# A planned attention-and-two-gated-layers kernel: the planner's costs are replaced, 157 due times are moved, k^T v is split by column halves, and two head pairs take the exponential of q row by row

## The chip, the cores and the metric

The kernel runs on one core of one Trainium2 chip. The metric is the device time of one execution in microseconds; lower is better. TensorE is PE in the rows, VectorE DVE, ScalarE ACT, GpSimd POOL and SyncE, which only issues DMAs here, SP.

## The reference

Linear attention over 4 batches, 8 heads, 576 positions and 64 columns, then two gated layers over the 2304 rows by 512 columns that come out of it, each with 1536 inner columns. Inputs of the attention are float32; the weights are 64-bit floats, so the kernel loads two 32-bit words for each weight and converts them.

```python
def _attn_ref(q, k, v):
    q_s = np.exp(q - np.max(q, axis=-1, keepdims=True))
    q_s = q_s / (np.sum(q_s, axis=-1, keepdims=True) + 1e-09)
    k_s = np.exp(k - np.max(k, axis=2, keepdims=True))
    k_s = k_s / (np.sum(k_s, axis=2, keepdims=True) + 1e-09)
    kv = np.einsum('bhsd,bhse->bhde', k_s, v)
    return np.einsum('bhsd,bhde->bhse', q_s, kv)
def _moe_ref(x, w_gate, w_val, w_out):      # first layer
    g = x @ w_gate
    return (g / (1.0 + np.exp(-g)) * (x @ w_val)) @ w_out
def _moe2_ref(x, w_a, w_b, w_out):          # second layer
    return ((x @ w_a) * (x @ w_b)) @ w_out
```

## The kernel before, in words

**Work.** A unit of attention is one batch and one pair of heads: u = 4 b + g, 16 units, written by `attend(b, g, ...)`. A unit loads k, q and v (512 main positions as 4 rows per partition, and 64 rest positions), takes the column maximum of k (transposes `kx` and `kb` on PE, a reduce on DVE), subtracts it, takes the exponential, multiplies k^T v on PE (`kv`, line 730: 4 matmuls of 130 columns for the main positions and one for the rest, both heads side by side), divides it by its sums (lines 737 to 751) and puts it into a block-diagonal matrix. q has its row maximum subtracted, its exponential taken and is divided by the row sums; it is turned on PE (`qt`, `ql`, lines 780 and 783), and `xt` and `xl` (lines 793 and 803) are the products with the block-diagonal matrix, the layer's input x.

For batch 0 (b == 0) q's maximum is subtracted on POOL (lines 698 and 702), one ACT instruction takes the exponential of k and q together (line 706, 1280 columns), DVE sums q's rows (line 756) and POOL divides (line 767). For the other batches ACT takes the exponential of q row by row: 9 instructions of line 717, each with the maximum as its bias and each followed by a read of its accumulator that gives the row's sum; POOL divides (lines 771 and 774).

**Weights.** The inner columns are cut into 12 tiles f of 128. `convert` turns the two words of each weight into one float32 in the tiles `a` (ACT lines 412 and 417; DVE lines 414 to 428; line 433 on DVE, where it is CUSTOM_DVE_ANT_0 in a profile and ISA in an order, or on POOL, where it is a TENSOR_TENSOR), and then into a high part (ACT line 438) and a low part (the helper `pair`, line 326, on DVE or POOL): the tile `w`, called w0_f for layer 0. A float32 product is made of three: low times high, high times low, high times high.

**Blocks.** Layer 0 runs over block 0 (512 rows of batch 0; tile `xhl`, split into its high and low part) and block 1 in the plain way: for each f two products `u` (gate and value, lines 844 and 859, 12 matmuls each), SiLU on ACT into `s`, the product on DVE (line 873), its high part `h` on ACT and low part on DVE, and 12 matmuls into `acc` (line 886) that trail by one tile. Units of batch 1 are attended between block 0's products, those of batches 2 and 3 between block 1's. The rest of layer 0, and all of layer 1, runs in three supers over pairs of blocks (lines 1138, 1222, 1248, 1250, 1257), where sums of halves of x and of w are multiplied. The second layer's weights are converted in block 1's and the first supers' time (`convert_late`, tiles `latewr`).

**What sets the order.** Nothing is issued when it is written: `plan.add` records each operation with an engine, a cost in microseconds, what it reads and writes, and for some a second engine with a cost of its own. `prepare` gives each operation a due time, backwards from its successors. `order` then simulates the engines: at each step it takes, of the operations that can start first, the one that is due first; an operation with two engines goes to the second where that ends no later. `HOP` and `SAME` are the delays between engines and on one, `DMA_*` the model of a load, `TABLE` of a load of ACT's tables. `search` runs this 160 times, moving about 3% of the due times by up to 3 us at random, and keeps the shortest plan. `emit` issues in the order of that plan, so the engine queues and SP's DMAs stand in it; the semaphores come from the data. The products of the layers are chained (`product`), so that their own order is fixed; what moves are the attention's PE operations between them, everything on DVE, ACT and POOL, the choice between DVE and POOL or ACT, the buffers and the loads.

Of the kernel before, what the change touches and what calls it, by code (L numbers as in the profile page):

```python
# [31 lines left out]
class Plan:  # L32
# [58 lines left out]
    def hop(self, first, then, other):  # L91

        if first != then:
            return other
        return 0.0 if first == "tensor" else self.SAME

    def prepare(self):
# [7 lines left out]
        for n in reversed(range(len(ops))):  # L105
# [4 lines left out]
            for s in self.succ[n]:  # L110
                if n in ops[s]["hold"]:
                    continue
                hop = self.hop(op["engine"], ops[s]["engine"], self.SLACK) + lands if n in ops[s]["deps"] else 0.0
                t = min(t, self.due[s] - hop)
# [5 lines left out]
    def order(self):  # L120
# [37 lines left out]
        while len(done) < len(ops):  # L158
# [25 lines left out]
            if port:  # L184
                port_free = t + cost
# [8 lines left out]
            free[engine] = t + cost  # L194
# [13 lines left out]
            for s in succ[n]:  # L208
                left[s] -= 1
                if not left[s]:  # L210
                    at = ops[s]["engine"]
                    is_ready(s, max([end[d] + self.hop(ops[d]["runs"][run[d]][0], at, self.HOP)
# [4 lines left out]
    def search(self):  # L217

        self.prepare()
        rng, best = random.Random(0), None  # L220
        for n in range(self.ROUNDS):
            kept = self.due
            if best:
                self.due = [d + rng.uniform(-3, 3) if rng.random() < 0.03 else d for d in kept]
            try:
                found = self.order()
            except RuntimeError:
                self.due = kept
                continue
            if best and self.length > best[0]:  # L230
                self.due = kept
            else:
                best = self.length, found
        return best[1]

    def emit(self):
        done, run, slot = self.search()
# [7 lines left out]
def kernel(  # L245
# [90 lines left out]
    def dma(fn, nbytes, reads, writes, due=None, after=(), issue=0.475, queue="sync", hold=()):  # L336
# [5 lines left out]
    def load(fn, nbytes, writes, issue=0.475):  # L342
# [4 lines left out]

    mats = [[m.bitcast(U32) for m in ms] for ms in ((w_gate, w_val, w_out), (w_a, w_b, w_out2))]
# [4 lines left out]
    TOP = 122880.0  # L353
    LEAST = 2.0 ** -15
# [102 lines left out]
    def convert_late(f, m):  # L457
# [23 lines left out]
        dma(get, P * 2 * WH * 8, [], [LOW, HIGH], issue=0.95 if m < 2 else 0.475, after=first)  # L481
# [46 lines left out]
    def attend(b, g, xhl, due):  # L528
# [63 lines left out]
        def qraw():  # L592
            return col(Q, q0, n)
# [781 lines left out]
```

## Time and profile before

| | |
|---|---|
| time, median of 3 runs | 942.72 us (940.71 to 944.29) |
| the profiled execution's own time | 941.4 us |
| its span | 939.2 us, so 2.2 us lie around the span |
| PE busy | 904.6 us, 4400 matmuls |
| DVE, ACT, POOL busy | 638.1, 518.3, 334.9 us |

A busy PE is counted from the start to the modelled end of each matmul, and matmuls overlap; so the starts of rows that follow each other tell more than their durations. POOL's spans are rough.

### The profile page before, as it was taken

The page shows a single profiled execution, that of the slowest core. Times are in us where ns is not written, and L with a number is a line of the kernel's source. Part 1 is how long each engine was busy: PE and PEld are TensorE (multiplying, and loading weights), DVE is VectorE, ACT ScalarE, POOL GpSimd, SP SyncE. Part 2 cuts the span into 40 slices and gives each one's busy share as a digit, 9 for nine tenths or more (in the row PEclk, how much of TensorE's full clock was granted, in tenths as well). Part 3 has the DMA queues.
Part 4 walks back from the last instruction along what each step waited for, and adds up shares of the span by engine and source line. Part 5 has one row for each costly group of instructions (what it writes and reads, how often), then busy time and mean ns, then how long its engine had stood idle before and what let it go on. Part 6 is the DMA issues. An engine that isn't in the chain of part 4 may idle for free.

```text
span 939.2 us, 12787 instructions
## 1 busy us (share of the span) xinstructions
PE 904.6 (96%) x4400; PEld 753.0 (80%) x4400; DVE 638.1 (68%) x1025; ACT 518.3 (55%) x1020; POOL 334.9 (36%) x323
## 2 busy tenths in 40 slices
PE   5599999999999999999999999999999999999998
PEld 3477777788887888888888888888888888888886
DVE  6999996544376887877778665875796444564444
ACT  4798876878675665455464546443644453333310
POOL 6534221212052322435555633442565113242210
PEclk9989999999999999999999999999999999999999
DMA  9858765464327555354322753422223210110003
GB/s 271 273 204 263 237 224 192 122 195 131 88 90 234 157 147 156 120 165 154 112 91 72 228 183 101 135 89 90 68 66 115 79 46 22 45 46 23 23 1 112
DMA packets 108153, 121.42 MB, mean 129 GB/s; under 512 B 31929, under 2 KB 83897, under 8 KB 107961
## 3 DMA queue, kind: packets, MB, share of 16 engines
q1 hardware_dynamic: 102424, 116.55, 39.7%
q10 hardware_dynamic: 5664, 4.07, 1.4%
q8 instruction: 34, 0.56, 0.2%
q14 instruction: 31, 0.25, 0.1%
HBM read 88.60 MB, written 31.98 MB: 128 GB/s over the span
## 4 chain that ended last, share of the span: by engine, by line
PE 83%; DVE 5%; ACT 4%; DMA 3%; issue 2%; SPq 1%; POOL 1%; ACTq 0%; DVEq 0%; POOLq 0%
PE p L1138 35%; PE o L1248 15%; PE u L859 10%; PE q L1222 7%; PE o L1250 6%; PE acc L886 5%; PE o L1257 2%; DMA wr<-in_moe_w_out_dram 1%; PE xt L793 1%; DVE l2w L326 1%; ACT ut L717 1%; ACT a L412 1%; PE kv L732 1%; SPq L620 1%; DMA wf<-latewr 1%
## 5 line engine op out<-in xcount | busy, mean ns | idle before, releaser
L1138 PE MATMUL p<-l2w,l2w 128*128 128x512 f32 x1512 | 352.8, 389 | 1.2 <-DVE temps L326 1.2
L1138 PEld LDWEIGHTS p<-l2w,l2w 128*128 128x128 f32 x1512 | 283.1, 188 | 61.2 <-DVE temps L326 2.5
L859 PE MATMUL u<-xhl,w 128*128 128x512 f32 x552 | 143.3, 407 | 5.0 <-DVE w L326 4.8
L326 POOL TENSOR_TENSOR l2w<-raww,l2w 128x512 fp32r<-128x512 f32 x68 | 97.2, 1434 | 94.1 <-ACT l2w L333 94.0
L333 ACT CAST l2w<-raww 128x512 fp32r<-128x512 f32 x144 | 87.9, 621 | 74.9 <-PE p L1138 39.7
L859 PEld LDWEIGHTS u<-xhl,w 128*128 128x128 f32 x552 | 101.9, 191 | 31.8 <-DVE w L326 7.1
L326 DVE TENSOR_TENSOR sums<-o,sums 128x512 f32<-128x512 f32 x120 | 82.3, 689 | 53.2 <-PE o L1248 39.4
L326 DVE TENSOR_TENSOR temps<-p,temps 128x512 f32<-128x512 f32 x90 | 62.1, 690 | 67.1 <-PE p L1138 65.9
L1248 PE MATMUL o<-l2w,hp 128*128 128x512 f32 x288 | 97.0, 391 | 0.6 <-DVE sums L326 0.6
L1150 ACT COPY temps<-p 128x512 f32<-128x512 f32 x72 | 42.4, 588 | 67.3 <-PE p L1138 67.1
L326 DVE TENSOR_TENSOR l2w<-raww,l2w 128x512 fp32r<-128x512 f32 x76 | 57.1, 762 | 26.5 <-ACT l2w L333 26.3
L886 PE MATMUL acc<-h,w 128*128 128x512 f32 x288 | 72.1, 395 | 0.0
L1222 PE MATMUL q<-rest,l2w 128*128 128x256 f32 x432 | 65.4, 283 | 0.0
L1248 PE MATMUL o<-l2w 128*128 128x512 f32 x192 | 64.4, 389 | 0.0
L1248 PEld LDWEIGHTS o<-l2w,hp 128*128 128x128 f32 x288 | 53.4, 188 | 12.6 <-DVE sums L326 1.9
L886 PEld LDWEIGHTS acc<-h,w 128*128 128x128 f32 x288 | 52.9, 188 | 10.6
L1222 PEld LDWEIGHTS q<-rest,l2w 128*128 128x128 f32 x432 | 58.6, 192 | 0.9
L1250 PE MATMUL o<-hp,l2w 128*128 128x512 f32 x144 | 48.6, 391 | 1.4 <-DVE sums L326 1.4
L1248 PE MATMUL o<-l2w,l2w 128*128 128x512 f32 x168 | 49.6, 389 | 0.0
L1250 PE MATMUL o<-l2w 128*128 128x512 f32 x144 | 48.3, 389 | 0.0
L498 POOL TENSOR_TENSOR latewr<-latewr 128x512 uint32<-128x512 uint32 x17 | 24.0, 1413 | 61.5 <-DVE latewr L493 52.7
L326 POOL TENSOR_TENSOR raww<-raww,spare 128x512 f32<-128x512 f32 x15 | 20.1, 1341 | 68.7 <-DVE l2w L326 63.2
(197 smaller groups left out, 1470.9 us busy)
## 6 DMA issues: line engine op xcount, KB each, us to landing
raww<-wf SPq DMA_DIRECT2D x36, 512.0 KB, 4.3
raww<-wf SPq DMA_DIRECT2D x36, 256.0 KB, 3.4
wf<-latewr SPq DMA_DIRECT2D x36, 256.0 KB, 3.2
wf<-a SPq DMA_DIRECT2D x16, 384.0 KB, 2.7
latewr<-in_moe_w_a_dram SPq DMA_DIRECT2D x24, 256.0 KB, 2.9
latewr<-in_moe_w_b_dram SPq DMA_DIRECT2D x24, 256.0 KB, 3.7
latewr<-in_moe_w_out_dram SPq DMA_DIRECT2D x12, 512.0 KB, 5.0
wr<-in_moe_w_gate_dram SPq DMA_DIRECT2D x22, 256.0 KB, 2.9
```

Of the source, the lines that this page charges most:

```text
L326: engine.tensor_tensor(out=out(), in0=x(), in1=y(), op=op)
L333: add("scalar", act_us(n), lambda: nc.scalar.copy(out=hi(), in_=src()), src_keys, [hi_key])
L412: add("scalar", act_us(e) + 0.08, lambda rows=rows, halves=halves: nc.scalar.activation(out=a(halves).bitcast(F32), in_=rows()[..., 1].bit ...
L498: engine.tensor_tensor(out=u32(), in0=u32(), in1=r()[..., 0], op=ALU.add)
L859: nc.tensor.matmul(ps()[:, 0:n], lhsT=wv[:, c, :], rhs=x()[:, xs, c, 0:n], start=(a == 0 and c == 0), stop=(a == 2 and c == KD - 1))
L886: nc.tensor.matmul(ps()[:, 0:n], lhsT=w()[:, 4 + ws, o * P:(o + 1) * P], rhs=h()[:, hs, 0:n], start=begin, stop=end)
L1138: nc.tensor.matmul(ps()[:, 0:width], lhsT=wv(o)[:, m, ws, c, :], rhs=ops_x[o][xs][1]().rearrange("p (c n) -> p c n", c=2)[:, c, 0:width], ...
L1150: add("scalar", act_us(n), lambda: nc.scalar.copy(out=to[1]()[:, 0:n], in_=ps()[:, 0:n]), [ps], [to[0]], due=main["at"] + main["soon"])
L1222: nc.tensor.matmul(ps[m]()[:, 0:256], lhsT=wv(o)[:, m, ws, c % 2, :], rhs=rest_x[xs][1]().rearrange("p (c n) -> p c n", c=KD)[:, c, :], st ...
L1248: nc.tensor.matmul(ps(), lhsT=lhs(i, hs), rhs=outs_w[i][1]()[:, ws * 512:(ws + 1) * 512], **ends)
L1250: nc.tensor.matmul(ps()[:, 0:width], lhsT=outs_w[i][1]()[:, ws * 512 + r * P:ws * 512 + (r + 1) * P], rhs=hs2[i][t][1]()[:, hs * 512:hs * ...
L1257: nc.tensor.matmul(ps()[:, o * 256:(o + 1) * 256], lhsT=outs_w[i][1]()[:, ws * 512 + at:ws * 512 + at + P], rhs=rest_h[1]()[:, (2 * i + hs ...
```

## The change

Three things. First, the planner's numbers: delays between engines that depend on which they are, shorter issue and other load times, costs that let an engine's next operation start a little before the end of the last (`OVER`, `PORT`), other costs for single operations; and instead of the search, one run of `order` after 157 due times, listed by operation number in `MOVES`, have been moved by the listed microseconds. Second, `kv` is written as 10 matmuls of 65 columns instead of 5 of 130: each head's 64 columns of k are the stationary operand, at the column position 0 or 64, and the output holds the heads on its two partition halves. DVE's operations on it become one column wide, and its two scalings may go to ACT. Third, in batch 0 the head pairs g = 1 and g = 3 (`BYROW`) take the exponential of q row by row, as the other batches do; for g = 0 and 2 the division by the row sums may run on ACT as 10 instructions instead of one on POOL.

```diff
-    SAME, HOP = 0.1, 0.17
+    SAME, HOP, TO_TENSOR, TO_GPSIMD, FROM_TENSOR = 0.033, 0.06, 0.055, 0.1, 0.2
+    OVER = dict(vector=0.08, scalar=0.115, gpsimd=0.045)
+    PORT = 0.08
-    DMA_START, DMA_END, DMA_RATE, DMA_LANES = 1.1, 1.5, 290e3, 8
-    TABLE = 1.3
+    DMA_START, DMA_END, DMA_RATE, DMA_LANES = 1.0, 1.35, 393e3, 8
+    TABLE = 1.43
-    ROUNDS = 160
+    MOVES = (
+        5, 30, 6, 94.2, 8, 224.2, 9, 32.1, 27, 5.3, 32, 78.5, 36, -137.3, 39, 10.6, 50, -0.6, 55, 22.2, 58,
...
-                port_free = t + cost
+                port_free = t + cost - self.PORT
...
-            free[engine] = t + cost
+            free[engine] = t + cost - self.OVER.get(engine, 0.0)
...
     def emit(self):
-        done, run, slot = self.search()
+        self.prepare()
+        for n, us in zip(self.MOVES[::2], self.MOVES[1::2]):
+            self.due[n] += us
+        done, run, slot = self.order()
...
+        rows = b > 0 or g in BYROW
+        flat = b > 0 or g in FLAT
...
-        if b == 0:
+        if not rows:
             add("gpsimd", pool_us(m, BROADCAST), lambda: nc.gpsimd.tensor_tensor(
                 out=qx(), in0=qraw()[:, 0:m].rearrange("p (h r d) -> p r h d", h=HG, r=R),
...
-        pk, ks = psum([P, HG, D1], "kv"), small([P, 2, HG], "ks")
+        pk, ks = psum([P, D1], "kv"), small([P, 2], "ks")
 
         def kv():
-            for r in range(R):
-                nc.tensor.matmul(pk(), lhsT=kx()[:, r, :], rhs=vx()[:, :, r, :], start=(r == 0), stop=False)
-            nc.tensor.matmul(pk(), lhsT=kl(), rhs=vg()[:, G:G + 1, :].to_broadcast([P, HG, D1]),
-                             start=False, stop=True)
-
-        add("tensor", 1.3, kv, [K_, KL, *VS, VL, (C, "ones")], [pk])
+            for r in range(R + 1):
+                for h in range(HG):
+                    lhs, rhs = (kx()[:, r, rest_cols(h)], vx()[:, h, r, :]) if r < R else (kl()[:, rest_cols(h)], vg()[:, G, :])
+                    nc.tensor.matmul(pk()[rest(h), :], lhsT=lhs, rhs=rhs, start=r == 0, stop=r == R,
+                                     tile_position=(0, h * D))
+
+        add("tensor", KV, kv, [K_, KL, *VS, VL, (C, "ones")], [pk])
...
-        if b == 0:
+        if not rows:
             add("gpsimd", pool_us(n, BROADCAST), lambda: nc.gpsimd.tensor_tensor(
                 out=qg(), in0=qg(), in1=st()[:, 3, :].unsqueeze(2).to_broadcast([P, GX, D]), op=ALU.mult),
-                [*QS, st], QS)
+                [*QS, st], QS, other=("scalar", GX * (act_us(D) - 0.115) + 0.115, lambda: [nc.scalar.mul(
+                    out=qg()[:, x], in_=qg()[:, x], mul=st()[:, 3, x:x + 1]) for x in range(GX)], False))
```

The lines of the changed kernel are higher by 6 to 20; the rows below name the same operation by its own line. What the new order looks like at three places:

On ACT, from the first copy of kb to the copies of the rest of v, at the program's start (ut_92, ut_98, ut_103 and ut_105 or ut_106 are the units of batch 0). Before:

```order
L677 COPY kb_140<-kb_134 128x128
L677 COPY kb_148<-kb_144 128x128
L706 ACTIVATE ut_92<-ut_92 128x1280
L677 COPY kb_183<-kb_172 128x128
L706 ACTIVATE ut_98<-ut_98 128x1280
L654 COPY ut_92<-rests 128x64
```

And in the change:

```order
L689 COPY kb_143<-kb_138 128x128
L689 COPY kb_148<-kb_145 128x128
L729 ACTIVATE ut_98,st_140<-ut_98,st_140 128x64
L729 ACTIVATE ut_98,st_140<-rests,st_140 128x128
L729 ACTIVATE ut_98,st_140<-ut_98,st_140 128x64
L718 ACTIVATE ut_92<-ut_92 128x1280
L689 COPY kb_181<-kb_173 128x128
L729 ACTIVATE ut_98,st_140<-ut_98,st_140 128x64 x6
L782 ACTIVATE ut_92<-ut_92,st_128 128x64 x10
L689 COPY kb_227<-kb_219 128x128
L666 COPY ut_92<-rests 128x64
```

The exponential of the second unit's q has become nine row instructions, and the ten of line 782 are the division of the first unit's q, which stood on POOL.

On PE, where tile 0's products end and tile 1's begin (kx and kb are the transposes of the first unit of batch 1). Before:

```order
L844 MATMUL u_0_0_1_404<-xhl_0_302,w_0_332 128x512 x3
L669 MATMUL kx_459<-ident,tm_455 128x128 x2
L669 MATMUL kx_459<-ident,ut_394 128x128
L674 MATMUL kb_484<-ident,kr_478 128x128
L859 MATMUL u_0_1_0_494<-xhl_0_302,w_1_466 128x512 x12
L859 MATMUL u_0_1_1_534<-xhl_0_302,w_1_466 128x512 x12
L886 MATMUL acc_0_553<-h_0_0_503,w_0_332 128x512 x3
```

And in the change:

```order
L681 MATMUL kx_487<-ident,ut_431 128x128
L686 MATMUL kb_508<-ident,kr_504 128x128
L861 MATMUL u_0_0_0_425<-xhl_0_324,w_0_339 128x512 x3
L861 MATMUL u_0_0_1_435<-xhl_0_324,w_0_339 128x512 x3
L861 MATMUL u_0_0_0_425<-xhl_0_324,w_0_339 128x512 x3
L861 MATMUL u_0_0_1_435<-xhl_0_324,w_0_339 128x512 x3
L746 MATMUL kv_565<-ut_431 64x65 x10
L876 MATMUL u_0_1_0_584<-xhl_0_324,w_1_469 128x512 x12
L797 MATMUL qt_608<-ident,ut_431 128x128 x4
L876 MATMUL u_0_1_1_618<-xhl_0_324,w_1_469 128x512 x12
L903 MATMUL acc_0_639<-h_0_0_605,w_0_339 128x512 x3
```

Half of tile 0's products now stand behind kx and kb, and kv stands before tile 1's products instead of behind them.

On POOL, from the conversion of tile 4 on (a_4_0 is its first half; ut_705 and others are units of batch 1). Before:

```order
L433 TENSOR_TENSOR a_4_0_590<-a_4_0_590,wr_4_0_451 128x768
L326 TENSOR_TENSOR w_4_694<-a_4_0_590,w_4_694 128x3x256
L649 MEMSET ut_705 64x64 x4
L652 MEMSET ut_705 128x9
L771 TENSOR_TENSOR ut_476<-ut_476,st_573 128x512
L774 TENSOR_TENSOR ut_476<-ut_476,st_573 128x128
L433 TENSOR_TENSOR a_5_0_743<-a_5_0_743,wr_5_0_606 128x768
L649 MEMSET ut_843 64x64 x2
L326 TENSOR_TENSOR w_5_838<-a_5_0_743,w_5_838 128x3x256
```

And in the change:

```order
L443 TENSOR_TENSOR a_4_0_556<-a_4_0_556,wr_4_0_489 128x768
L785 TENSOR_TENSOR ut_523<-ut_523,st_603 128x512
L661 MEMSET ut_751 64x64 x2
L791 TENSOR_TENSOR ut_523<-ut_523,st_603 128x128
L661 MEMSET ut_751 64x64 x2
L664 MEMSET ut_751 128x9
L661 MEMSET ut_846 64x64 x4
L664 MEMSET ut_846 128x9
L443 TENSOR_TENSOR a_6_0_874<-a_6_0_874,wr_6_0_810 128x768
```

The low parts of w_4 and w_5 have gone to DVE, and so has line 443 for tile 5.

## Rows read from the trace of the kernel before

**Rows 1.** The page: busy time, share and count by engine.

```profile
PE 904.6 (96%) x4400; PEld 753.0 (80%) x4400; DVE 638.1 (68%) x1025; ACT 518.3 (55%) x1020; POOL 334.9 (36%) x323
```

**Rows 2.** Stages: PE, PEld, DVE, ACT, POOL busy (count), clock, DMA share, GB/s.

```profile
0.00:32.00 32.00, 18.38 (x95) 13.87 (x96) 22.79 (x56) 17.42 (x34) 21.89 (x36) 1.00 0.97 303
32.00:60.80 28.80, 19.88 (x82) 15.12 (x80) 28.01 (x35) 24.76 (x43) 11.13 (x17) 0.88 0.66 209
60.80:103.90 43.10, 40.10 (x190) 32.14 (x189) 40.44 (x65) 38.34 (x90) 16.39 (x21) 1.00 0.76 242
103.90:152.00 48.10, 47.09 (x215) 37.58 (x215) 45.46 (x68) 35.80 (x59) 9.55 (x12) 1.00 0.69 228
152.00:286.80 134.80, 134.54 (x655) 109.51 (x656) 72.44 (x160) 98.11 (x257) 32.89 (x67) 1.00 0.43 129
286.80:934.60 647.80, 644.60 (x3169) 544.82 (x3167) 428.28 (x646) 303.91 (x541) 243.06 (x171) 1.00 0.33 103
```

**Rows 3.** Waits of PE over the whole span: total, times, longest.

```profile
PE u L859 <- DVE w L326: 4.8, 4, 2.0
PE o L1250 <- DVE sums L326: 1.4, 2, 1.2
PE p L1138 <- DVE temps L326: 1.2, 2, 0.8
```

**Rows 4.** Timeline of PE: start, duration, instructions, idle time before.

```profile
47.20 7.86 PE L859 MATMUL u<-xhl,w 128*128 128x512 f32 x24 [1.42 <-DVE w L326]
54.90 2.88 PE L886 MATMUL acc<-h,w 128*128 128x512 f32 x12
57.62 1.05 PE L732 MATMUL kv<-ut 128*128 128x130 f32 x8
...
58.73 0.60 PE L780 MATMUL qt<-ident,ut 128*128 128x128 f32 x4
...
95.35 0.33 PE L803 MATMUL xl<-ut 128*128 128x64 f32 x2
95.49 2.09 PE L859 MATMUL u<-xhl,w 128*128 128x512 f32 x8
...
151.90 5.29 PE L859 MATMUL u<-xhl,w 128*128 128x512 f32 x22 [0.33 <-DVE w L326]
```

**Rows 5.** Groups of DVE by form in 0 to 152 us: busy, mean ns, idle before.

```profile
L326 DVE TENSOR_TENSOR w<-a,w 128x768 fp32r<-128x768 f32 x11 | 10.8, 983 | 0.0
L756 DVE TENSOR_REDUCE st<-ut 128x10 f32<-128x640 f32 x4 | 3.2, 811 | 1.6 <-ACT ut L706 1.6
L761 DVE TENSOR_SCALAR st<-st 128x9 f32<-128x9 f32 x4 | 3.0, 740 | 0.6 <-ACT ut L717 0.6
```

**Rows 6.** The last of these groups in 152 to 300 us.

```profile
L761 DVE TENSOR_SCALAR st<-st 128x9 f32<-128x9 f32 x8 | 1.4, 177 | 4.1 <-ACT ua L717 4.1
```

**Rows 7.** Timelines of POOL and DVE near 71 us.

```profile
71.20 2.08 POOL L326 TENSOR_TENSOR w<-a,w 128x768 fp32r<-128x768 f32 x1 [2.31 <-ACT w L438]
71.83 1.57 DVE L761 TENSOR_SCALAR st<-st 128x9 f32<-128x9 f32 x1 [0.24 <-ACT ut L717]
```

**Rows 8.** Waits of DVE in 0 to 152 us.

```profile
DVE kr L672 <- PE kx L669: 2.3, 2, 1.7
DVE u L873 <- PE u L859: 1.7, 3, 0.9
DVE st L756 <- ACT ut L706: 1.6, 1, 1.6
DVE xhl L326 <- ACT xhl L333: 1.1, 2, 0.6
```

**Rows 9.** Groups of ACT by form in 0 to 152 us.

```profile
L717 ACT ACTIVATE ut<-ut,st 128x64 f32<-128x64 f32 x32 | 10.9, 352 | 0.1
L717 ACT ACTIVATION_READ_ACCUMULATOR ut<-ut,st 128x1 f32 x36 | 7.2, 201 | 0.0
```

**Rows 10.** A wait of ACT in 0 to 61 us.

```profile
ACT kb L677 <- DMA rests<-in_q_dram: 6.0, 1, 6.0
```

More of the change, by code (lines that the diff above doesn't have):

```diff
@@ L1 @@
-import random
 from contextlib import ExitStack
@@ L89, in add, with hop @@
         return n
[L91 to L95, printed above, removed]
+    def hop(self, first, then):
+        if first == "tensor":
+            return 0.0 if then == "tensor" else self.FROM_TENSOR
+        return dict(gpsimd=self.TO_GPSIMD, tensor=self.TO_TENSOR).get(then, self.SAME)
     def prepare(self):
@@ L211, in order @@
                     at = ops[s]["engine"]
-                    is_ready(s, max([end[d] + self.hop(ops[d]["runs"][run[d]][0], at, self.HOP)
+                    is_ready(s, max([end[d] + self.hop(ops[d]["runs"][run[d]][0], at)
                                      for d in ops[s]["deps"]] + [issued[d] for d in ops[s]["order"]]))
@@ L215, in order, with emit @@
         return done, run, slot
-    def search(self):
+    def emit(self):
         self.prepare()
[L220 to L236, printed above, removed]
-        done, run, slot = self.search()
+        for n, us in zip(self.MOVES[::2], self.MOVES[1::2]):
+            self.due[n] += us
+        done, run, slot = self.order()
         for b, tag in slot.items():
@@ L334, in split, with dma, load @@
         pair(n, lo, src, lambda: hi().bitcast(F32), ALU.subtract, [*src_keys, hi_key], [lo_key], not psum, not psum)
-    def dma(fn, nbytes, reads, writes, due=None, after=(), issue=0.475, queue="sync", hold=()):
+    def dma(fn, nbytes, reads, writes, due=None, after=(), issue=0.37, queue="sync", hold=()):
         return add(queue, issue, fn, reads, writes, due=due, nbytes=nbytes, after=after, hold=hold)
     last_load, last_x, not_before = [], [], []
-    def load(fn, nbytes, writes, issue=0.475):
+    def load(fn, nbytes, writes, issue=0.51):
         n = dma(fn, nbytes, [], writes, after=last_load, issue=issue, hold=tuple(not_before))
@@ L353 @@
     TOP = 122880.0
+    KV = 0.94
     LEAST = 2.0 ** -15
@@ L480, in convert_late @@
         A1, LOW, HIGH = [(buf, (at, x)) for x in range(3)]
-        dma(get, P * 2 * WH * 8, [], [LOW, HIGH], issue=0.95 if m < 2 else 0.475, after=first)
+        dma(get, P * 2 * WH * 8, [], [LOW, HIGH], issue=0.95 if m < 2 else 0.37, after=first)
         add("scalar", act_us(2 * WH) + 0.08, lambda: nc.scalar.activation(
@@ L772, in attend @@
                 out=qx(), in0=qx(), in1=st()[:, 3, 0:G].rearrange("p (h r) -> p r h", h=HG).unsqueeze(3).to_broadcast(
-                    [P, R, HG, D]), op=ALU.mult), [*QS, (st, 3)], [Q_, *QS])
+                    [P, R, HG, D]), op=ALU.mult), [*QS, (st, 3)], [Q_, *QS],
+                other=("scalar", G * (act_us(D) - 0.115) + 0.115, lambda: [nc.scalar.mul(
+                    out=qx()[:, r, h], in_=qx()[:, r, h], mul=st()[:, 3, h * R + r:h * R + r + 1])
+                    for r in range(R) for h in range(HG)], False) if b in NORM else None)
             add("gpsimd", pool_us(P, BROADCAST), lambda: nc.gpsimd.tensor_tensor(
@@ L1294, in out_chunk @@
                     dma(lambda at=at, row=row: nc.sync.dma_start(out=row, in_=to[1]()[at, :]),
-                        P * DM * 4 // len(rows), [to[0]], [], due=main["at"] + 10)
+                        P * DM * 4 // len(rows), [to[0]], [], due=main["at"] + 10,
+                        issue=0.37 if len(rows) < 2 else 0.56)
         chunks = [lambda k=k: out_chunk(k) for k in range(2 * R + 2 * rested)]
```

60 lines of the change are left out of this document (33 added, 27 removed), and 17 rows, old and new, of the table MOVES.

## The prediction

> **What bounds the kernel now.** I read the busy times first: PE is busy 904.6 of 939.2 us and no other engine over 68% [rows 1], so over the whole span PE is the bound and a gain must come out of the time in which it waits or runs slowly. The table of stages tells where that is [rows 2]. In the three supers PE is busy for 644.6 of 647.8 us, in block 1 for 134.54 of 134.80; in 0 to 32 us it is busy for 18.38 only, in 32 to 60.8 us for 19.88 of 28.8 at a mean clock of 0.88, and up to 152 us it still misses 3.0 and 1.0 us. So what can be won lies mostly in block 0.
>
> Next, who is waited for there. PE waits 4.8 us, in four waits, for a low part of w that DVE makes [rows 3]. And the DVE column of the stages is full: 28.01 of 28.8, 40.44 of 43.1, 45.46 of 48.1 us [rows 2]. The last of the four ends at 151.90 us, after 0.33 us, before the products of tile 11, the last of block 0 [rows 4]; in the 48.1 us up to there PE was busy for 47.09. So in this stretch PE and DVE run level: **when block 0 ends is set by when DVE has worked off what stands ahead of the last low part of w**. DVE was busy for 22.79 + 28.01 + 40.44 + 45.46 = 136.7 us of the first 152 and idle for 15.3 [rows 2]. The early slow place (tile 1's 24 products take 54.90 - 47.20 = 7.7 us, where 12 products take 57.62 - 54.90 = 2.72 later, so 24 take 5.44 [rows 4]) costs PE 2.3 us, but PE meets DVE again afterwards, so that these are hidden unless DVE also gets faster.
>
> **Block 0: DVE's queue.** From the order I counted what stands on DVE up to and with the last low part of w_11: 220 instructions before, 225 after. By kind: 4 more low parts of 768 columns, 4 x 0.98 = +3.9 [rows 5]; two more pairs of 512 columns, +1.4; one less each of line 433's two forms, half and whole tile, about -1.0 and -1.8; two less row sums of 811 ns, -1.6 [rows 5], since g = 1 and 3 get these sums from ACT; three more scalings, +0.8; the rest +0.2. Sum **+1.9 us**: row-wise exponentials take work from DVE, but the low parts that come over from POOL are more. (Terms without a row here are mostly one instruction each, priced by a like operation; I put an error of 1 us on them together.)
>
> What DVE loses beside POOL. At 71.83 us a DVE instruction on 9 columns takes 1.57 us; it ends just after POOL's low part, which runs from 71.20 for 2.08 us [rows 7]. Over the first 152 us this form takes 740 ns in the mean, later, where POOL does less, 177 [rows 5, 6]: this form alone loses 4 x 0.56 = 2.3 us, and others have no twin in the later stretch that would price them. POOL is busy for 21.89 + 11.13 + 16.39 + 9.55 = 59.0 us of the first 152 [rows 2]; of its five low parts of 768 columns four go, about 2.08 us each [rows 7], -8.3, while what else goes (two of batch 0's subtractions of each kind, three divisions) and comes (two row-wise divisions, one half and one whole tile of line 433) is nearly even. 8.3/59 of 2.3 is 0.3 us; as the low parts are the long ones and other forms suffer too I take **-1.5 us**, between 0 and twice the 2.3, -4.6.
>
> DVE's idle time, 15.3 us. Part of it is the first load and stays. Four waits, for kx 2.3, for a product of PE 1.7, for the exponential 1.6, for xhl 1.1, sum to 6.7 us [rows 8]. A plan with other delays and moved due times puts other ready work there; two of the four sums that waited for the exponential are gone, and PE's tile 0 products and kv stand elsewhere. That it comes out so is the choice that I can prove least: between 0 and -6.7 I take **-5.0 us**.
>
> Block 0 together: 1.9 - 1.5 - 5.0 = **-4.6 us**, between +2.9 (all of the first term, 1 us more of it, nothing else) and -9.4.
>
> ACT's part. 18 row instructions with their reads come, 18 x (0.352 + 0.201) = 10.0 us, two exponentials shrink to k's half, about -1, and ten small multiplies of 64 columns come, at most 3.5 by the row of that width [rows 9]; about +11. ACT was busy for 17.42 + 24.76 = 42.2 us of the first 60.8 [rows 2], so it would be at 53: costed at nothing, hidden in ACT's 18.6 idle us. Without this cover it is a rival, below. The loads stand in nearly the same order on SP up to the second unit of batch 1, so I let their time stand.
>
> **kv.** Ten matmul rows take 58.73 - 57.62 = 1.11 us per unit now [rows 4]. After it there are 20 of 65 columns. The nearest row is xl, 64 columns: two in 95.49 - 95.35 = 0.14 us, so 0.07 each [rows 4]. One behind the other that is 1.4 us (+0.29 per unit), both halves at once 0.7 us (-0.41). Only the 8 units inside block 1 are on PE's path for certain, so -3.3 to +2.3 us; I take a middle **-0.5**. The Trainium skill, TensorEngine Tiling (Array Packing), section Theoretical Speedup, gives up to 2x where the stationary operand has at most 64 columns; by that alone the term would be -3.3 and the sum below 2.8 us lower. Its section Key Properties also says that changing the tiling mode drains TensorE, which speaks against this edit; no row here shows such a switch.
>
> **Block 1 and the supers.** In block 1 PE lacks 0.3 us by its busy time [rows 2], and breaks between attention and products cost some more; **-1.0**, between -2 and +2, as DVE has 62 and ACT 37 us free there. In the supers the order shows the same 3168 matmul instructions in the same order, so only waits can go or come: o and p wait 1.4 + 1.2 = 2.6 us in the two longest lines [rows 3]. I take **-2.0**, between -2.6 and +4: some 18 low parts of supers' weights go over from POOL to DVE, which is busy for 428 of 648 us there and POOL for 243 [rows 2], and a late one would make a new wait.
>
> **Sum.** -4.6 - 0.5 - 1.0 - 2.0 = -8.1 us. The profiled execution took 941.4 us (span 939.2 and 2.2 around it), so 933.3. The median of the runs is 1.3 us above the profiled one; I say **933.5**.
>
> **Rivals.**
> - *PE is rid of DVE in block 0.* DVE's idle time and what it loses beside POOL shrink more than I take, and PE runs through from tile 2 on. To be had at most: 8.9 us idle in 32 to 60.8 us, the 2.3 us at the low clock, 4.0 us idle up to 152 us [rows 2, 4], 15.2 us. For it: all of it waits on orders that a plan can change. Against: the DVE sum rises by 1.9. Two thirds of it, -10, with the other terms -3.5: 928.
> - *Nothing comes of it.* DVE's waits come back elsewhere, its longer queue eats the rest: block 0 between 0 and -2, kv serial at +2.3, supers 0 to +2: about 941. For it: DVE is full either way, and a plan's gain in block 0 is taken back wherever one operation comes later than planned.
> - *ACT becomes late (slower).* Place: tile 0's SiLU and the high part of h_0_0, for which acc_0 waits on PE (54.90 us before [rows 4]). If the row instructions don't fall into ACT's idle time but behind its waits, all that follows on ACT comes 11 us later, and acc_0 at 66; of this PE gets back its later waits, 4.8 us for w [rows 3]: +6.2 us, and 947.6 without the other terms, 944 with them. It decides from 8.3 us of lateness, 4.8 and 3.5: below that the kernel is still not slower. For it: ACT at 53 of 60.8 us leaves 8 for all waits. Against: the rows of g = 1 need only the load of q and its maximum, and stand in the order before the long waits for POOL, in the 6.0 us in which ACT waited for the rests before its first copy of kb [rows 10].
> - *PE empties at each kv*. If PE lets a product run out before the first 65-column matmul and again behind the last, it loses what a matmul overlaps its follower: 54.90 + 2.88 - 57.62 = 0.16 us [rows 4]. 8 units x 2 x 0.16 = +2.6 in block 1: 936. This is within the forecast's own range, so it has no chance of its own. The drain of the Trainium skill's TensorEngine Tiling (Array Packing), Key Properties, would be this.
>
> **Chances.** The forecast (927 to 938) 0.55, PE free of DVE (922 to 928) 0.20, nothing (938 to 943) 0.17, ACT late (943 to 950) 0.08. The range that leaves out no more than 2 in 10 is 923 to 941. About 0.5% (4.7 us) is what a measurement of this kernel can tell from no change: faster by more than that, below 938, 0.76; within it 0.18; slower 0.06.
>
> **What would show it.** Right: the wait for the last w of block 0 ends near 147 us instead of 151.9; DVE idle up to there near 10 us; kv rows between 0.7 and 1.4 us per unit; acc_0 starts by 56 us; block 1's and supers' lengths within 3 us of 134.8 and 647.8. Wrong: DVE idle still 15 us; acc_0 beyond 58 us with ACT named as what it waited for; a new wait over 2 us in the supers; or block 0's end before 143 us, which would be the first rival.

## The result and the profile after

The changed kernel takes **953.93 us** (median of 4 runs, 950.68 to 956.37) against 943.15 us for the kernel before on the same chip; the ratio is 1.0116 (95% interval 1.0077 to 1.0154). It is slower by about 11 us where I forecast 933.5. The profiled execution has a span of 953.2 us, 14.0 longer than before.

The page's line of busy times, and the table of stages with the columns of [rows 2], cut where the same places of the program stand now:

```profile
PE 910.4 (96%) x4560; PEld 746.2 (78%) x4560; DVE 649.9 (68%) x1053; ACT 521.8 (55%) x1061; POOL 294.4 (31%) x293
```

```profile
151.50:287.83 136.33, 133.71 (x735) 104.92 (x735) 77.35 (x168) 95.93 (x254) 28.32 (x64) 1.00 0.45 134
287.83:948.60 660.77, 650.05 (x3169) 545.70 (x3167) 438.39 (x661) 304.15 (x542) 215.55 (x152) 0.99 0.32 99
```

The last row is the result: the supers take 660.8 us instead of 647.8 [rows 2], 13.0 of the 14.0 us. Up to the first p, at 287.83 instead of 286.8 us, the two kernels differ by 1 us. The matmuls of the supers and their order are the same, so PE waits or runs slowly there. Its four lines of waits in the supers sum to 10.6 us instead of 3.2: that is 7.4 of the 13.0 us. About 2.5 more are one stretch at a lower clock, shown below with e11, and some 3 us lie in small steps and are not located. The two longest lines (total, times, longest):

```profile
PE p L1155 <- DVE temps L332: 5.9, 3, 3.4
PE p L1155 <- ACT temps L1167: 2.5, 4, 0.9
```

p waits because the bank of an earlier p has not been emptied: `temps` are the copies and sums that take p out of it, on ACT and DVE. So the next question is what ACT and DVE were doing. Their waits for DMA in the supers, in the changed kernel (loads, and in `wf<-latewr` the store of a converted weight, whose place in the buffer is to be written again):

```profile
ACT l2w L339 <- DMA raww<-wf: 22.4, 7, 4.9
ACT latewr L496 <- DMA latewr<-in_moe_w_a_dram: 7.0, 5, 2.2
...
DVE latewr L494 <- DMA wf<-latewr: 8.1, 4, 3.6
```

and in the kernel before:

```profile
ACT l2w L333 <- DMA raww<-wf: 2.7, 2, 2.4
...
DVE latewr L484 <- DMA wf<-latewr: 1.1, 1, 1.1
```

With the lines left out, ACT stood 47.0 us for DMA instead of 5.5, and DVE 19.5 instead of 3.2; in the change 8.9 of the 66.5 us are for stores, and I count them with the loads below. These engines take their instructions in order, so whatever stands behind the one that waits is late too. One place shows the whole chain. ACT's timeline (start, duration, instruction, idle time before it):

```profile
366.58 0.58 ACT L1171 ACTIVATE temps<-p 128x512 f32<-128x512 f32 x1
369.25 0.67 ACT L496 ACTIVATE latewr<-latewr 128x512 uint32<-128x512 uint32 x1 [2.09 <-DMA latewr<-in_moe_w_a_dram]
...
370.33 0.58 ACT L1167 COPY temps<-p 128x512 f32<-128x512 f32 x1
```

and PE's:

```profile
361.77 8.32 PE L1155 MATMUL p<-l2w,l2w 128*128 128x512 f32 x36
370.96 1.42 PE L1155 MATMUL p<-l2w,l2w 128*128 128x512 f32 x5 [0.87 <-ACT temps L1167]
```

ACT stands 2.09 us for the load of a second layer's weight, which after its conversion only goes back to DRAM (`wf`); the copy of p behind it ends near 370.9, and PE waits for just that until 370.96.

Why do such instructions stand there? The change's planner counts 1.0 us, 393 KB per us and 1.35 us for a load or a store (`DMA_START`, `DMA_RATE`, `DMA_END`), so 1.0 + 0.67 + 1.35 = 3.0 us for 256 KB and 3.7 for 512 KB; the planner before counted 3.5 and 4.4. What they took (the page's DMA issues: count, KB, median us from issue to landing), after:

```profile
raww<-wf SPq DMA_DIRECT2D x36, 512.0 KB, 5.4
...
wf<-latewr SPq DMA_DIRECT2D x36, 256.0 KB, 4.2
```

and before:

```profile
raww<-wf SPq DMA_DIRECT2D x36, 512.0 KB, 4.3
...
wf<-latewr SPq DMA_DIRECT2D x36, 256.0 KB, 3.2
```

The second is the store. Both take longer than the new numbers say, by 1.7 and 1.2 us; before, the first was met and the second took 0.3 less than counted. Not every kind runs late: `raww`'s loads of 256 KB take 2.9 us for 3.0. The comparison is a rough one, since the planner adds the time that a transfer stands behind others, and these medians hold it. So my theory L: the new load numbers are too short, and what needs a load is put into the queues too early. The rival D is the one that my prediction had priced: DVE has more to do in the supers (438.4 us instead of 428.3). M is a third: the moved due times.

### The profile page after: what moved, and what is told of

Read it like the earlier page. It is cut to its first block, busy times and chain, and to the rows that moved or that the text cites. A ratio compares the mean times of both kernels' runs of the same rounds, so it can differ in the third digit from the quotient of the medians.

```text
span 953.2 us, 13140 instructions
## 1 busy us (share of the span) xinstructions
PE 910.4 (96%) x4560; PEld 746.2 (78%) x4560; DVE 649.9 (68%) x1053; ACT 521.8 (55%) x1061; POOL 294.4 (31%) x293
## 4 chain that ended last, share of the span: by engine, by line
PE 66%; DMA 10%; DVE 10%; ACT 6%; issue 3%; SPq 3%; POOL 1%; ACTq 0%; DVEq 0%; POOLq 0%
PE p L1155 28%; PE o L1265 14%; PE q L1239 7%; PE u L876 5%; PE o L1267 5%; PE acc L903 3%; DVE l2w L332 3%; DMA wf<-latewr 2%; DMA wr<-in_moe_w_out_dram 2%; PE o L1274 2%; DMA latewr<-in_moe_w_b_dram 2%; ACT ut L729 1%; DMA ut<-in_k_dram 1%; DVE temps L332 1%; DVE sums L332 1%
## 5 line engine op out<-in xcount | busy, mean ns | idle before, releaser
L332 POOL TENSOR_TENSOR l2w<-raww,l2w 128x512 fp32r<-128x512 f32 x57 | 79.0, 1387 | 106.6 <-ACT l2w L339 106.2
L332 DVE TENSOR_TENSOR l2w<-raww,l2w 128x512 fp32r<-128x512 f32 x87 | 68.6, 799 | 31.8 <-ACT l2w L339 31.3
L339 ACT CAST l2w<-temps 128x512 fp32r<-128x512 f32 x36 | 22.2, 620 | 43.0 <-PE o L1265 27.6
```

The lines of the kernel that those rows point to most:

```text
L332: engine.tensor_tensor(out=out(), in0=x(), in1=y(), op=op)
L339: add("scalar", act_us(n), lambda: nc.scalar.copy(out=hi(), in_=src()), src_keys, [hi_key])
```

## The experiments

All in one table. The first p and the end of the last matmul are read from PE's timeline, the supers are the difference; waits are those of ACT and of DVE for DMA in the supers. Times are medians, ratios are to the kernel before on the same chip. The last three columns come from one execution of each kernel. The four rows with the plan of before (before, e4, e9, e14) tell how far they can be trusted: their first p lies between 286.2 and 293.2 us, their supers between 647.2 and 647.8.

| run | us | ratio (95%) | first p | supers | ACT + DVE wait for DMA |
|---|---|---|---|---|---|
| before | 942.72 | | 286.8 | 647.8 | 5.5 + 3.2 |
| the change | 953.93 | 1.0116 (1.0077 to 1.0154) | 287.8 | 660.8 | 47.0 + 19.5 |
| e1_loads_supers | 946.60 | 1.0042 (1.0026 to 1.0059) | 287.3 | 652.3 | 25.7 + 8.2 |
| e1_loads_supers_late | 947.01 | 1.0053 (1.0036 to 1.0071) | 289.3 | 655.4 | 5.4 + 5.2 |
| e12_loads_from_200 | 943.05 | 1.0000 (0.9988 to 1.0012) | 287.3 | 649.2 | 18.3 + 5.9 |
| e15_loads_from_100 | 947.53 | 1.0057 (1.0039 to 1.0074) | 291.0 | 650.9 | 20.7 + 7.7 |
| e2_loads_all | 958.87 | 1.0174 (1.0160 to 1.0188) | 303.6 | 648.6 | 18.3 + 3.0 |
| e3_before_fast_loads | 957.52 | 1.0149 (1.0131 to 1.0167) | 300.4 | 651.8 | 31.1 + 12.6 |
| e5_no_moves | 969.25 | 1.0282 (1.0257 to 1.0308) | 292.9 | 671.5 | 59.5 + 21.8 |
| e6_before_planner | 951.20 | 1.0096 (1.0081 to 1.0110) | 297.7 | 646.4 | 15.4 + 3.9 |
| e8_before_seed | 945.69 | 1.0039 (1.0025 to 1.0053) | 290.5 | 648.6 | 6.7 + 2.9 |
| e10_before_rows | 946.41 | 1.0039 (1.0026 to 1.0052) | 291.4 | 648.6 | 7.7 + 4.0 |
| e4_before_kv | 942.27 | 1.0001 (0.9991 to 1.0011) | 290.0 | 647.2 | 6.8 + 4.0 |
| e9_kv_block1 | 939.49 | 0.9962 (0.9948 to 0.9976) | 286.2 | 647.4 | 7.1 + 1.7 |
| e14_before_kv_b1 | 943.56 | 1.0019 (1.0004 to 1.0034) | 293.2 | 647.2 | 6.7 + 2.9 |
| e11_after_old_kv | 950.58 | 1.0071 (1.0055 to 1.0086) | 288.5 | 655.7 | 46.0 + 19.5 |
| e13_loads_and_kv | 943.96 | 1.0019 (1.0007 to 1.0031) | 288.1 | 648.9 | 18.5 + 6.7 |

**The load numbers in the changed kernel.** In e1_loads_supers `order` counts the loads that it starts after 284 us of its plan by the numbers of before:

```diff
-                dma_free = max(dma_free, t + self.DMA_START) + op["nbytes"] / self.DMA_RATE
-                end[n] = dma_free + self.DMA_END
+                start, stop, rate = (1.1, 1.5, 290e3) if t > 284 else (self.DMA_START, self.DMA_END, self.DMA_RATE)
+                dma_free = max(dma_free, t + start) + op["nbytes"] / rate
+                end[n] = dma_free + stop
```

> The changed kernel, whose planner counts the loads that start after 284 us of its plan with the numbers of before (1.1 us, 290 KB per ms-thousandth, 1.5 us) and all else as changed; the plan up to there, and so block 0 and block 1, stay as they are. Theory L (the new load numbers put instructions that need a load too early into the queues of ACT and DVE, which stand there, and the copies of p behind them come late): the supers fall from 660.8 to 648 to 654 us, ACT's and DVE's waits for loads there from 47 and 20 us to less than half, the time to 942 to 947. Theory D (DVE has more to do in the supers, 438 instead of 428 us, and is late for p): this plan gives DVE 663 operations there instead of 661, so the supers stay above 657 and the time above 949.

The supers fell to 652.3 us and the time by 7.3, while DVE had as much to do there as in the change. D's forecast, above 657, is off. The waits fell from 66.5 to 33.9 us in all, ACT's by a little less than the half that L had named. Its supers (columns of [rows 2]):

```profile
287.30:939.60 652.30, 645.27 (x3169) 544.54 (x3167) 437.45 (x664) 305.24 (x544) 208.26 (x148) 1.00 0.32 101
```

e1_loads_supers_late has `(1.1, 3.5, 290e3)` in the same place.

> As the run before, but each load after 284 us counted to land 2 us later still. Theory L: waits of ACT and DVE for loads in the supers under 10 us together, the supers at 646 to 650 us, the time 940 to 944. Theory D: DVE gets 668 operations there, 7 more than in the changed kernel, so the supers are above 658 us.

The waits all but went (10.6 us, where L had under 10), but the supers are longer than in e1: 655.4 us, where L had 646 to 650, with DVE busy for 436. So L in its simple form (fewer waits, shorter supers) is not enough. Against the kernel before, matmul by matmul, e1 and this run have both lost 4.2 us by 330 us, and this run 3 us more near 700 us: counted too long, the loads put the weights themselves late, and PE waits for those (2.0 us for l2w in its rows, which the changed kernel's do not have):

```profile
PE p L1156 <- DVE temps L333: 2.1, 2, 1.9
PE p L1156 <- DVE l2w L333: 2.0, 2, 1.3
```

e12_loads_from_200 has `t > 200` for `t > 284`.

> As the first run (loads counted by the numbers of before), but for all loads that start after 200 us of the plan instead of 284, so that those of block 1's second half which the supers' first products need are counted so too. In the first run DVE still waited 2.3 us near 297 us for a load planned before 284, and PE waited for it at 303 to 323 us, 4.9 us in three places. Theory L: these waits are gone as well, the supers at 647 to 651 us, the time 942 to 945. Theory D (DVE's work): no change against the first run, supers 651 to 654.

The supers took 649.2 us and the time came out level with the kernel before. DVE was busy for as long as in the change and POOL for less:

```profile
287.30:936.50 649.20, 644.82 (x3169) 544.68 (x3167) 438.21 (x671) 304.90 (x544) 202.75 (x145) 1.00 0.32 103
```

By 330 us e12 has lost 0.2 us against the kernel before and not 4.2, so the early loss of the two runs above hung on how the loads planned between 200 and 284 us are counted. This takes all of the 11 us back with three numbers, and D is out. ACT still stood 18.3 us for loads, but PE waited 1.4 us for copies of p instead of 8.4; it is not the sum of the waits that counts but what stands behind them:

```profile
PE p L1156 <- DVE temps L333: 1.0, 1, 1.0
PE p L1156 <- ACT temps L1168: 0.4, 1, 0.4
```

**The load numbers in the kernel before.** e3_before_fast_loads is the kernel before with one line of the change:

```diff
-    DMA_START, DMA_END, DMA_RATE, DMA_LANES = 1.1, 1.5, 290e3, 8
+    DMA_START, DMA_END, DMA_RATE, DMA_LANES = 1.0, 1.35, 393e3, 8
```

> The kernel before with nothing but the four load numbers of the change (1.0 us, 393, 1.35 us), its own search kept. Theory L: ACT and DVE wait for loads in the supers for over 20 us instead of 8.5, the supers are 651 to 660 us instead of 647.8, the time 945 to 954. Theory D: DVE gets 632 operations there, 11 less than before, so the supers are 646 to 649 us and the time 940 to 944.

L's forecast for the waits and the supers came out (43.7 us of waits, 651.8); the time is beyond its range, since the first p starts 13.6 us later too, which L had not named. Up to there ACT waits 26.0 us for DMA instead of 13.3 and DVE 19.3 instead of 9.3, so the numbers seem to do harm in block 0 and 1 as well; how much of the 13.6 us that is, one plan can't tell. In the supers they cost 4.0 us here and 13.0 in the change, so the size of the loss depends on the rest of the plan. Over all runs, the supers take 646.4 to 652.3 us in plans that count their loads by the old numbers (655.4 where 2 us are added) and 651.8 to 671.5 in plans that count them by the new ones.

**The moved due times, and chance.** e2_loads_all has the old load numbers everywhere in the changed kernel (in the due times too, which e1, e12 and e15 leave alone), e5_no_moves an empty `MOVES`, e15_loads_from_100 `t > 100`.

> The changed kernel with the four load numbers of before for all loads. Theory L: supers 648 to 654 us, as in the first run, and in block 0 the waits of DVE for what ACT and loads deliver shrink too, so that the first p starts at 284 to 288 us; time 939 to 946. Theory D: DVE gets 671 operations in the supers, 10 more than in the changed kernel; supers above 658. A third theory, M (the 157 moved due times fit only the plan for which they were listed): anything that changes the plan makes block 0 longer, first p later than 290 us.

> The changed kernel with an empty list of moved due times: the plan that the new numbers give by themselves. Theory L (new load numbers too short): ACT and DVE wait for loads in the supers as in the changed kernel, over 40 us together, and the supers are 655 to 663 us, so the time 953 to 962. Theory M (the moved due times do the harm): supers 647 to 652, and the time below 948.

> As the run with the load numbers of before from 200 us of the plan on, but from 100 us on. Theory L alone: 941 to 944, DVE's waits for loads in block 1 shorter than 7.9 us. Theory M (the moved due times fit the plan that they were listed for): the plan of block 0's end and of block 1 changes, the first p starts at 289 us or later, supers as in the other run, the time 945 or more.

The supers behave as L says in e2 and e15 (648.6 and 650.9 us); the times do not (958.87 and 947.53, where L had at most 946 and 944). In e5 they are 671.5, beyond the 655 to 663 of L. M, that the moved due times do the harm, is wrong: without them the kernel is 15 us slower still, 10.7 of them in the supers, a gain of the moved due times there that neither theory had. But M's other half holds as far as it goes: they fit one plan. Where the load numbers change the plan of block 0 (e2) or of its end and block 1 (e15), the first p comes 15.8 and 3.2 us later, though the supers are the shorter ones by these numbers. The 3.2 us alone would lie within the spread of first p; e15's time is 4.5 us above e12's.

Three more kernels change the plan in other ways. e6_before_planner has the class `Plan` of before, and all else as changed. The other two are the kernel before, e8_before_seed with the first of these edits and e10_before_rows with the second (and `rows` for each test of b in q's part):

```diff
-        rng, best = random.Random(0), None
+        rng, best = random.Random(1), None
...
+        rows = b > 0 or g in (1, 3)
-        if b == 0:
+        if not rows:
```

> The kernel before with another seed of its search: how far the time of a plan depends on chance alone. If the loss of 11 us in the change or the 15 us of the load numbers could be chance, this run is off by over 5 us as well; I expect the supers within 3 us of 647.8 and the time at 938 to 948.

> The changed kernel's k^T v, its row-wise exponentials and its costs of single operations, under the planner of before: its delays, its load numbers, its 160 rounds of search, no moved due times. Theory L: the supers are 646 to 651 us again, ACT and DVE wait for loads there less than 15 us together; the time 938 to 946. If the row-wise exponentials cost time by themselves: block 0 ends later than 153 us though the planner is the old one.

> The kernel before with the row-wise exponential of q for g = 1 and 3 and nothing else; its planner, costs and search as before, so the plan is another one by its search too (another seed alone made 4 us). If the row-wise exponentials cost time by themselves, by what ACT has more to do before tile 0's SiLU: the first acc product starts later than 57 us and block 0 ends later than 155 us, the time 946 to 952. If they are hidden in ACT's idle time: block 0 ends at 150 to 155 us and the time is 940 to 946.

With the old planner the supers are short again (646.4 us; the waits, 19.3 us, are above the 15 that L had named), so k^T v, the rows and the single costs do not by themselves make the supers longer. In block 0 and 1 this plan is 10.9 us longer than that of before: tile 11's products, the last of block 0, start at 157.95 us (150.96 before), which was the sign named for a cost of the rows. How much of it is chance can't be told: another seed alone moved the first p by 3.7 us and the time by as much. The row-wise exponentials alone came to 946.41, no more than what the seed did; the first acc product started at 54.8 us, as before [rows 4], so ACT was not late there. But tile 11's products started at 156.7 us (154.6 with the other seed), a little later than the 155 named for hidden rows. Their own cost is within chance, and stays open.

**k^T v.** e4_before_kv has the new `kv` in the kernel before, in an unchanged plan. e9_kv_block1 has it only for batches 2 and 3, e14_before_kv_b1 with `b >= 1` in its place:

```diff
-        pk, ks = psum([P, HG, D1], "kv"), small([P, 2, HG], "ks")
+        halves_kv = b >= 2
+        pk, ks = psum([P, D1] if halves_kv else [P, HG, D1], "kv"), small([P, 2, HG], "ks")
...
+            if halves_kv:
+                for r in range(R + 1):
```

e11_after_old_kv is the change with the old `kv`, its plan untouched; e13_loads_and_kv is e12 with the new `kv` only where `b >= 2`.

> The kernel before with k^T v by column halves and nothing else: the plan, its costs and its search are those of before, so each engine's order is the same but for the ten matmuls. In the changed kernel's trace twenty 65-column matmuls took 0.80 us where the eight and two of before took 1.11, 0.31 us less per unit. If the halves run beside each other here too, block 1 is 8 x 0.31 = 2.5 us shorter and the time 939 to 941.5; if PE has to be empty at each change, about 1.0 us per unit and no difference that can be measured, 941.5 to 944; if it makes DVE's or ACT's work behind kv slower, longer than before.

> The kernel before with k^T v by column halves for batches 2 and 3 only, whose units are attended in block 1; the plan is that of before. With the halves for all units (the run of the kernel before with them) kv took 5.86 us in block 1 instead of 8.50, but the granted clock was below full in four stretches of the first 112 us instead of one, and the time the same. Theory C (in block 0 the shorter kv is paid back by a lower clock, in block 1 not): the clock rows of the first 152 us are those of before, block 1 is 2 to 3 us shorter, the time 939 to 940.5. If the gain of kv is taken back in block 1 itself (PE then waits there for DVE): 941 to 943.

> The kernel before with k^T v by column halves for batches 1 to 3, 5 matmuls of 130 columns for batch 0 alone. If the clock of the first 32 us, in which PE has little else to do than batch 0's attention, is what the halves cost (theory C): as with halves in batches 2 and 3 alone, the time 938 to 940.5, no stretch at the low clock near 30, 63 or 108 us. If the cost comes from batch 1's kv, between block 0's products: 941 to 943.5.

> The changed kernel with k^T v as 5 matmuls of 130 columns; its plan is not touched. If the column halves are worth what their rows say, 0.31 us in each of 8 units, block 1 is 2.5 us longer and the time 955 to 958. Theory C (the shorter kv is paid back by the clock in block 0): the stretches at the low clock in the first 62 us get fewer and block 0 ends 1 to 3 us earlier, so that the time is 952 to 955.

> The changed kernel with the load numbers of before from 200 us of its plan on (943.05 us as it was run), and k^T v by column halves only for batches 2 and 3, in 5 matmuls of 130 columns for batches 0 and 1. If what the halves cost in block 0 and what the loads cost in the supers add up, the 3.5 us between the two runs of the kernel before with halves everywhere and with halves in block 1 come off: 938 to 941. If block 0 is bound here by DVE alone, whatever k^T v takes: 942 to 944.

One unit of block 1, first in the kernel before and then in e9:

```profile
214.31 1.07 PE L859 MATMUL u<-xhl,w 128*128 128x512 f32 x4
215.22 1.05 PE L732 MATMUL kv<-uc,ua 128*128 128x130 f32 x8
216.11 0.38 PE L733 MATMUL kv<-uc,ua 128*128 128x130 f32 x2
216.33 0.33 PE L783 MATMUL ql<-ident,ua 128*128 128x64 f32 x2
```

```profile
214.50 1.07 PE L872 MATMUL u<-xhl,w 128*128 128x512 f32 x4
215.50 0.80 PE L737 MATMUL kv<-uc,ua 128*64 128x65 f32 x20
216.23 0.43 PE L796 MATMUL ql<-ident,ua 128*128 128x64 f32 x2
```

From kv's start to the next row it is 0.73 instead of 1.11 us, but the four products ahead of it take 1.00 instead of 0.91: 0.29 us are left of 0.38. In the kernel before, with halves for batches 2 and 3 alone, this is worth 3.3 us by the medians, and **e9 is faster than both kernels**, than the one before by 0.4% (its profiled execution is only 1.0 us shorter than the one of before, so the rest is not located). With halves for batch 1 too (e14) or for all (e4), nothing of it is left. My theory C said that this is the clock of the first 32 us, in batch 0's attention. e14 has the old kv there and no low clock there, and loses all the same (its time is just above the 941 to 943.5 us named for batch 1's kv); so C as I put it is wrong. What differs is later in block 0. The stages of e14, and then of e9:

```profile
120.00:132.00 12.00, 10.20 (x41) 7.96 (x41) 8.96 (x11) 7.48 (x12) 2.04 (x1) 0.86 0.81 267
152.00:164.00 12.00, 10.15 (x37) 7.84 (x37) 5.98 (x10) 2.71 (x6) 0.58 (x4) 0.86 0.67 218
```

```profile
120.00:132.00 12.00, 11.29 (x57) 9.05 (x55) 11.53 (x15) 9.36 (x15) 1.85 (x1) 1.00 0.80 275
152.00:164.00 12.00, 11.69 (x53) 9.57 (x53) 5.28 (x11) 6.76 (x20) 3.33 (x8) 1.00 0.52 169
```

and PE in e14 at the two places:

```profile
123.07 1.21 PE L806 MATMUL xt<-ut 128*128 128x512 f32 x2 [1.80 <-ACT ut L800]
...
156.57 6.92 PE L872 MATMUL u<-xhl,w 128*128 128x512 f32 x22 [1.85 <-DVE w L326]
```

The xt wait is 0.70 us in e9, and the clock stays at 1.00. In e14 PE waits 1.80 and 1.85 us, and runs at a lower clock behind each. Why ACT and DVE are later there in a plan that is the same is not shown; e14's runs also lie further apart than the others' (940.64 to 947.97 us), so that the profile is one of several courses. In the changed kernel it is another matter: e13 does not gain over e12 (943.96 and 943.05), so the parts do not add up, and e11 does gain 3.3 us over the change, below both of its forecasts (952 at the least), and in the supers (655.7 instead of 660.8), not in block 0.

That difference is one place. DVE in the changed kernel, and then in e11:

```profile
560.94 0.43 DVE L494 TENSOR_SCALAR latewr<-latewr 128x512 uint32<-128x512 uint32 x1 [1.94 <-DMA latewr<-in_moe_w_b_dram]
...
564.61 1.56 DVE L508 CUSTOM_DVE_ANT_0 latewr<-latewr 128x1024 uint16<-128x1024 uint16 x1
566.09 1.75 DVE L332 TENSOR_TENSOR l2w<-raww,l2w 128x512 fp32r<-128x512 f32 x1
...
568.36 0.68 DVE L332 TENSOR_TENSOR temps<-p,temps 128x512 f32<-128x512 f32 x1
```

```profile
564.87 0.69 DVE L508 CUSTOM_DVE_ANT_0 latewr<-latewr 128x1024 uint16<-128x1024 uint16 x1
565.48 0.69 DVE L332 TENSOR_TENSOR l2w<-raww,l2w 128x512 fp32r<-128x512 f32 x1
...
567.40 1.73 DVE L332 TENSOR_TENSOR temps<-temps 128x512 f32<-128x512 f32 x1
```

and POOL and PE in the changed kernel, their timelines and the stages there (columns of [rows 2]):

```profile
563.88 3.42 POOL L332 TENSOR_TENSOR l2w<-raww,l2w 128x512 fp32r<-128x512 f32 x2
```

```profile
569.09 2.93 PE L1155 MATMUL p<-l2w,l2w 128*128 128x512 f32 x6 [3.39 <-DVE temps L332]
```

```profile
569.09:574.40 5.31, 5.31 (x13) 4.15 (x14) 2.91 (x6) 1.91 (x3) 0.00 (x0) 0.50 0.43 134
574.40:580.00 5.60, 5.60 (x26) 4.64 (x25) 3.19 (x6) 3.03 (x6) 2.44 (x2) 0.99 0.76 233
```

DVE stands 1.94 us for a load and has no idle time of note from there to `temps`. Beside two low parts of POOL (563.88 to 567.30 us) two of its instructions take 3.31 us instead of 1.38, `temps` comes late, PE waits 3.39 us, and then issues 13 matmuls in 5.31 us at a clock of 0.50, nearly twice the time that the next take: about 6 us in one place. In e11 DVE waits 0.59 us for that load, POOL starts its pair at 565.74 and meets another instruction of DVE, and PE, 1.9 us further back by then, does not wait. So about 6 of the 13.0 us hang on this place, and a small shift in time undoes it: e11 has 65.5 us of waits for DMA as against 66.5, and loses about 1 us more elsewhere. The change's four runs lie between 950.68 and 956.37 us, so it may not come in each of them. e1 and e12, with other loads, do not have it either.

## Why the prediction was wrong

**The step that failed is the one on the loads.** "The loads stand in nearly the same order on SP ..., so I let their time stand" looked at the order of the issues in block 0 and not at what stands behind them on the engines that consume them, and for the supers I did not ask it at all. I had read the new load numbers in the diff and gave them no term. The supers' term, -2.0 (-2.6 to +4), was bounded by DVE's extra low parts; it measured +13.0. The sign that I named for it, a new wait over 2 us in the supers, came (3.39 us), but in the main through waits for DMA on ACT and DVE, which e12 takes back at the same DVE load. A slip besides: 933.3 and the 1.3 us of the median make 934.6 and not 933.5, which changes nothing here.

**What bounds block 0** was right: PE waits for the last low parts of w here too, 0.90 us for the one before the last, and DVE is nearly full up to there. The last one ends at 151.47 us instead of 151.84. DVE in the change, and then before:

```profile
149.65 1.82 DVE L332 TENSOR_TENSOR w<-a,w 128x768 fp32r<-128x768 f32 x2
```

```profile
150.89 0.95 DVE L326 TENSOR_TENSOR w<-a,w 128x768 fp32r<-128x768 f32 x1
```

PE in the change, and its stage up to the third product of tile 11, which starts behind that last low part, at 151.52 instead of 151.90 us [rows 4]:

```profile
150.66 4.34 PE L876 MATMUL u<-xhl,w 128*128 128x512 f32 x16 [0.90 <-DVE w L332]
```

```profile
0.00:151.52 151.52, 126.67 (x658) 95.62 (x658) 133.52 (x225) 121.72 (x265) 50.52 (x77) 0.97 0.77 245
```

The term of -4.6 measured -0.4. DVE's busy time fell from 136.6 to 133.5 us where I had +1.9 - 1.5 = +0.4: if the count of +1.9 stands, the loss beside POOL was mis-sized, about -5.0 instead of -1.5, a little beyond the bound of -4.6. The idle time, "the choice that I can prove least", went the other way: 18.0 us instead of 15.3, where I took -5.0. That was one of my signs of being wrong. DVE's longest waits up to there:

```profile
DVE a L429 <- ACT a L422: 3.6, 5, 1.9
DVE tm L332 <- DMA ut<-in_k_dram: 3.5, 1, 3.5
DVE st L703 <- DMA ut<-in_q_dram: 2.1, 2, 1.8
DVE st L774 <- ACT ut L729: 1.6, 2, 1.2
```

The waits for kx and u [rows 8] are all but gone, and new ones stand in their place: for ACT's part of the weights' conversion, and for q's load.

**ACT late** was right in its place and wrong in its price: acc_0 started at 58.71 instead of 54.90 us, behind two waits of PE for SiLU of 1.9 us together. PE had this back by tile 6, whose products start at 100.5 us (101.2 before). What more ACT had to do shows in the 3.6 us above, which DVE waited for it.

**kv** was right: 0.73 us from its start to the next row, near the 0.7 for halves side by side, and it costs 0.09 in the products ahead of it. The Trainium skill, TensorEngine Tiling (Array Packing), Theoretical Speedup, gives up to 2x, and the trace agrees: 20 matmuls of 65 columns at 0.037 us against 0.07 for xl [rows 4]. The 0.09 us at the way in may be the drain that its section Key Properties names; no row shows one at the way out. Before, kv takes 1.03 or 1.11 us to the next row, by what that is, so eight units are worth 8 x 0.21 to 0.29, about 2 us. Yet **block 1** got longer by 1.4 us (151.52 to 287.83 against 151.90 to 286.77): PE waited 2.4 us there instead of 0.3, longest for a division on POOL, and over 1 us more is not located:

```profile
PE qt L797 <- POOL ua L785: 1.1, 1, 1.1
```

**The chances.** I gave 0.06 to slower. Two unpriced things lay outside my cases: a planner that believes its loads to be faster than they are, and plans whose times differ by 3 to 4 us for no reason but the draw.

## What to carry to other kernels

Where a planner fixes the order of engines that work in order, an estimate that is too short can be dear (15 us in e3): an engine that waits for a load holds up all that stands behind it, here the copies that PE needs. Compare each number of the model with the landing times of a trace, and where a change makes the model faster, ask first what stands behind each instruction that reads a load. And when a plan is made anew, let another seed show how much of a difference is the draw before giving it to an edit.

## What the runs showed of the hardware

Two DVE instructions took 3.31 us beside POOL, and 1.38 in e11, where POOL's pair starts 0.26 us into the second of them. There the next instruction with both inputs in SBUF, temps<-temps, took 1.73 us instead of 0.69, while the two between them that read p took 0.69 and 0.68. The Trainium skill, SBUF — State Buffer, section Who interferes with whom, says that a DVE instruction with two SBUF inputs contends with a GpSimd instruction that reads SBUF; the low part l2w, with 1.75 against 0.69 us, agrees.

Waits of PE of 1.80, 1.85 and 3.39 us were each followed by a stretch at a lower clock: after the longest, 13 matmuls ran at 0.50, that is at 1.2 GHz, while the next stretch stands at 0.99, and in e14 the 22 products behind the wait of 1.85 us took 6.92 us, where 22 took 5.29 at full clock [rows 4]. There the wait and what followed cost 1.7 to 1.9 times the wait. But others of that length were followed by the full clock: 2.16 us ahead of 104.31 us in e14, and in the kernel before 1.99 us ahead of this stretch (columns of [rows 2]):

```profile
103.87:108.00 4.13, 4.13 (x18) 3.43 (x19) 3.94 (x8) 4.13 (x14) 0.00 (x0) 1.00 0.87 271
```

What decides it is not shown. And matmuls on half of the columns cost the matmul ahead of them 0.09 us.
